# Spreading the transposes, splitting the first products and issuing half of the stores from ScalarE in a convolution with spectral mixing

## The chip, the cores and the metric

The kernel runs on one core of one Trainium2 chip. The metric is the device time of one execution in microseconds. A core has five engines that run their own instruction streams (TensorE for matmuls, VectorE, ScalarE, GpSimd, and SyncE, which issues DMAs here) and 16 DMA engines that move data between the chip's memory (HBM) and the on-chip memory (SBUF). Matmul results are held in PSUM, in 8 banks.

## The reference

The input `x` is float32 of 8 batches x 3264 positions x 192 channels. A causal convolution along the positions (7 taps, softmaxed weights, 8 heads of 24 channels) gives `x'`. A spectral layer keeps the 64 lowest modes, mixes the channels of each mode with a complex 192 x 192 matrix, and goes back. Then comes a residual with a relu:

```python
out = einsum('hk,bskhg->bshg', softmax(weight), windows(x_padded))   # the convolution
X = rfft(out, axis=1)[:, :64]
Yr = Xr @ w_r - Xi @ w_i ;  Yi = Xr @ w_i + Xi @ w_r                 # mode by mode
u = out + irfft(Y, n=S)
result = u + maximum(u @ w_ch, 0)                                    # float32, 8 x 3264 x 192
```

## The kernel before

The 3264 positions are cut into 27 windows of 122 (`WIN`), with 128 rows loaded for each. The whole input is kept in SBUF as bfloat16 (`x_all`), and the convolution overwrites it in place.

Up to about 67 us the kernel loads `x`, convolves it (L243, L250, L252) and computes the 64 modes of the transform by matmuls with a table of sines and cosines, `fst` (L263, L275). All loads are issued by GpSimd[...].

The middle stage is the loop over 16 groups of four modes (`NGRP`, L561). `load_weights(g)` fetches a group's two weight blocks (L234); there are three buffers for this from group 7 on, so that the load of group g + 3 is issued when `mix(g)` is done. `mix(g)` multiplies the modes with the weights (L422) and ScalarE copies the result out (L426). `mix_t(g)` transposes it (L432) into `yeT` (L433). Between the two stands other TensorE work. `t_next` does a pair of chunks of transposes of the convolved input (L389), 22 pairs in all, which VectorE and ScalarE copy to the stashes `cTa` and `cTb` (L393, L395); `make_tail` (L350) prepares the rows for it. `g_part` (L405 to L410) does the same for the sine table and makes `gst`. Groups 0 to 7 have two pairs each, groups 8 to 13 one pair. In front of the mix of group 14 stand four calls of `ab_full` (L469, L474), which begin the accumulation of the first four units in the four PSUM banks of `pza`.

Then `zw_part` (L445) multiplies the mixed modes with the channel matrix, `g_full` (L464) and `relu` (L506) finish the first four units, and the final loop (L610) makes all others. A unit is one window of two batches: `(h, w, k)`, with half `h` of the batches, window `w` and pair `k`. Each unit has a "first half" and a "second half" of its first products on two row tiles of TensorE (`z_ops`, L484), a relu on ScalarE in PSUM (L506), the products of the inverse transform (`y_ops`, L501) and VectorE's addition of `x_all` into an output tile `t` (L536, `finish_unit`). The steps are staggered: at step j of the loop unit j has its first half, j - 2 its second half and relu, j - 4 and j - 5 their `y_ops`, and j - 5 its addition. Each step waits for the PSUM bank of the unit eight before (four before in the first steps). When both pairs of a window and half are added, SyncE stores the tile (L546): 393,216 bytes in rows of 768. There are eight tiles `t` (pool `p3`).

The order of the units is a list: window 0 of the first half, then alternately the next window of the first half and the window before it of the second half:

```python
    wq = [(0, worder[0])]
    for i in range(1, NWIN):
        wq.append((0, worder[i]))
        wq.append((1, worder[i - 1]))
    wq.append((1, worder[-1]))
```

The instructions stand on each engine in the order in which the program writes them.

Of the kernel before, what the change touches and what calls it, by code (L numbers as in the profile page):

```python
# [18 lines left out]
def kernel(  # L19
# [9 lines left out]
    nc = tc.nc  # L29
# [9 lines left out]
    NWIN = 27  # L39
# [5 lines left out]
    NGRP = MODES // MG  # L45
# [17 lines left out]
    def load_unit(b, u):  # L63
# [9 lines left out]
        else:  # L73
# [22 lines left out]
                      in_=bass.AP(tensor=weight.tensor, offset=weight.offset, ap=[[0, P], [1, H * KK]]))  # L96
# [26 lines left out]
    for g in range(4):  # L123
        i0 = OV if g == 0 else 0
        nc.vector.tensor_copy(out=diagc[32 * g:32 * g + 32, i0:NB],
                              in_=diag[32 * g:32 * g + 32, 32 * g - OV + i0:32 * g + 32])
# [46 lines left out]
    for g in range(4):  # L173
        i0 = OV if g == 0 else 0
        dst = cband[32 * g:32 * g + 32, :, 32 * g - OV + i0:32 * g + 32]
# [55 lines left out]
    def load_weights(g, pool):  # L231
        wt = pool.tile([P, MG, 3, D], BF16, tag="wt", name="wt")
        for half, src in ((0, moe_w_r), (1, moe_w_i)):
            nc.gpsimd.dma_start(out=wt[64 * half:64 * half + 64, :, :, :],  # L234
                                in_=src[MG * g:MG * g + MG, :, :].rearrange("m (p j) e -> p m j e", j=3))
        wtiles[g] = wt
# [127 lines left out]
    for p in range(4):  # L364
        k = 0
        for i in range(11):
            n = 8 if i < 4 else 7
# [5 lines left out]
    def ahead(i):  # L373
        for p, k, n in chunks[i:i + 2]:
            w0 = max(k - 2 * NWIN, 0)
            w1 = k + n - 2 * NWIN
            if w1 > w0:
                make_tail(p, w0, w1 - w0)
# [38 lines left out]
    def mix(g):  # L417
        zt = pt.tile([P, 512], F32, tag="p", name="yp")
        for j in range(3):
            for pos in range(4):  # L420
                m = MG * g + pos
                nc.tensor.matmul(zt[32 * pos:32 * pos + 32, 0:D],  # L422
                                 xt[:, j:j + 2, :, m].rearrange("p j k -> p (j k)"), wtiles[g][:, pos, j, :],
                                 start=(j == 0), stop=(j == 2), tile_position=(0, 32 * pos))
        ymix = workp.tile([P, D], BF16, tag="ymix")
        nc.scalar.copy(out=ymix[:], in_=zt[:, 0:D])  # L426
        return zt, ymix
# [34 lines left out]
    def g_full(u, zp, part):  # L462
        h, w, k = u
        nc.tensor.matmul(zp[:, 0:2 * D], gst[:, WIN * w:WIN * w + P], zwi[(h, part, k)], start=False,  # L464
                         stop=(part == 1), skip_group_check=True)

    def ab_full(u, zp):
        h, w, k = u
        nc.tensor.matmul(zp[:, 0:2 * D], xt[:, 3, 0:2, :].rearrange("p a m -> p (a m)"), win0[:, :],  # L469
                         start=True, stop=False, skip_group_check=True)  # L470
        for i in range(2):
            for c0, wv in ((WIN * (NWIN * i + w), win0[:, 0:D]),
                           (WIN * (2 * NWIN + w), (wB0[:, :], win1[:, 0:D])[i])):
                nc.tensor.matmul(zp[:, D * i:D * i + D], cTs[2 * h + k][:, c0:c0 + P], wv,  # L474
                                 start=False, stop=False, skip_group_check=True)
# [29 lines left out]
    def relu(zp):  # L505
        return nc.scalar.activation(out=zp[:, 0:2 * D], in_=zp[:, 0:2 * D], func=ACT.Relu)  # L506
# [24 lines left out]
    def finish_unit(u, zp):  # L531
        h, w, k = u
        if k == 0:
            ts[h] = p3.tile([P, B // 2, D], F32, tag="t", name="t")
        t = ts[h]
        add = nc.vector.tensor_tensor(  # L536
            out=t[:, 2 * k:2 * k + 2, :],
            in0=zp[:, 0:2 * D].rearrange("p (i e) -> p i e", i=2),
            in1=x_all[:, 4 * h + 2 * k:4 * h + 2 * k + 2, w, :], op=ALU.add)
        if k == 0:  # L540
            return
        rows = ((0, 80), (80, LASTVALID)) if w == NWIN - 1 else ((0, P),)
        for r0, r1 in rows:
            dst = bass.AP(tensor=out.tensor, offset=out.offset + (4 * h * S + WIN * w + r0) * D,
                          ap=[[D, r1 - r0], [S * D, B // 2], [1, D]])
            nc.sync.dma_start(out=dst, in_=t[r0:r1, :, :])  # L546


    CH = 7
    worder = sorted(range(NWIN), key=lambda w: (w % CH, w // CH))  # L550
    wq = [(0, worder[0])]
    for i in range(1, NWIN):
        wq.append((0, worder[i]))
        wq.append((1, worder[i - 1]))
    wq.append((1, worder[-1]))
    seq = [(h, w, k) for h, w in wq for k in range(2)]

    ahead(0)
    gq = [0, 1]
    zps = []  # L560
    for g in range(NGRP):  # L561
        last = g == NGRP - 1
        if g == 14:
            assert tpos[0] == len(chunks)
            zps = [pza.tile([P, 512], F32, tag="z", name="z") for _ in range(4)]
            for n in range(4):
                ab_full(seq[n], zps[n])
        m = mix(g)
        if g == 6:
            wts0_stack.close()  # L570
            cTb = ctx.enter_context(tc.tile_pool(name="stashb", bufs=1)).tile([P, CTW], BF16, tag="cTb")
            nc.vector.memset(cTb[:, NSLOT * WIN:CTW], 0.0)
            cTs[3] = cTb[:, :]
        if g in (0, 1, 2):
            load_weights(g + 7, wp)
        elif 7 <= g and g + 3 < NGRP:
            load_weights(g + 3, wp)
        if not last:
            for _ in range(2 if g < 8 else 1):
                t_next(2 if g < 6 else 3)  # L580
            if gq and g % 2 == 1:
                g_part(gq.pop(0))
        mix_t(g, *m)
    early_stack.close()
# [10 lines left out]
    for n in range(2):  # L595
        g_full(seq[n], zps[n], 1)
        finish_unit(seq[n], zps[n])
# [1 line left out]
        g_full(seq[n], zps[n], 0)  # L599
        relu(zps[n])  # L600
    zw_part(1, 1, "vv")
    for n in range(2, 4):
        g_full(seq[n], zps[n], 1)
        finish_unit(seq[n], zps[n])
    ps2.close()
    pzb = ctx.enter_context(tc.tile_pool(name="pzb", bufs=4, space=PSUM))

    N = len(seq)
    zword, yword = {}, {}
    for j in range(4, N + 6):  # L610
        o0, o1 = [], []
        if j < N:
            zps.append((pza if j % 8 >= 4 else pzb).tile([P, 512], F32, tag="z", name="z"))
            o0 = z_ops(seq[j], zps[j], 0)
        if 4 <= j - 2 < N:
            o1 = z_ops(seq[j - 2], zps[j - 2], 1)
        zword[j] = run_pair(o0, o1, zword.get(j - 2))
        if 4 <= j - 2 < N:
            relu(zps[j - 2])
        o0, o1 = [], []  # L620
        if 4 <= j - 4 < N:
            o0 = y_ops(seq[j - 4], zps[j - 4], 0)
        if 4 <= j - 5 < N:
            o1 = y_ops(seq[j - 5], zps[j - 5], 1)
        yword[j - 4] = run_pair(o0, o1, yword.get(j - 5))
        if 4 <= j - 5 < N:
            finish_unit(seq[j - 5], zps[j - 5])

# [1 line left out]
_INS = ['x', 'weight', 'moe_w_r', 'moe_w_i', 'moe_w_ch']  # L630
# [26 lines left out]
```

## Time and profile before

| what | value |
|---|---|
| median of 8 runs | 191.26 us (190.46 to 193.28) |
| the profiled execution | 191.18 us |
| its span, first to last instruction | 189.4 us |
| mean TensorE clock granted | 0.932 |
| TensorE, VectorE, ScalarE, GpSimd busy | 152.4, 126.7, 114.4, 49.3 us |
| issued by GpSimd: DMA packets' time as a share of 16 engines' span | 78.0% |
| issued by SyncE: the same | 36.4% |

The profile is of one execution. The span is shorter than the device time of the same execution by 1.8 us. PE stands for TensorE's matmuls, PEld for its weight loads, DVE for VectorE, ACT for ScalarE, POOL for GpSimd, SP for SyncE, SPq for SyncE's queue of instructions. L546 is line 546 of the kernel as printed above. A DMA share over 1 means that some of the 16 DMA engines had more than one packet in work.

### The profile page before, as it was taken

Reading aid. Unit: us, or ns where it says so; the run is one execution under the profiler, and the core shown is the slowest. Engines: PE = TensorE matmul, PEld = TensorE weight load, DVE = VectorE, ACT = ScalarE, POOL = GpSimd, SP = SyncE. Lnnn points to the kernel's source line nnn. Section 1 sums busy time; section 2 is a strip of 40 time slices with the busy share of each in tenths; the row PEclk is TensorE's granted clock in tenths of the full one; section 3 lists DMA queues with packets and bytes.
Section 4 is the critical chain, followed back from the end, with each engine's and each line's share of the span. In section 5 each row is a group of like instructions: output and inputs, shape, how many; then the busy total and the mean of one; then the engine's idle time right before and its main releaser. Section 6 shows DMA issues by size and latency. Waiting matters only on the chain.

```text
span 189.4 us, 5478 instructions
## 1 busy us (share of the span) xinstructions
PE 152.4 (80%) x2145; PEld 131.3 (69%) x2145; DVE 126.7 (67%) x257; ACT 114.4 (60%) x197; POOL 49.3 (26%) x77
## 2 busy tenths in 40 slices
PE   0637499888899787989849969999999999999800
PEld 0315389777787575868737747899999999998500
DVE  5988965625434358686734408699999999998900
ACT  2049945655575357668643416688888888888600
POOL 7957344332632843421445000000000000000000
PEclk9997969999999999999995599999999999999955
DMA  3999999999999999999999920599999999999996
GB/s 39 164 184 192 192 192 193 192 192 193 192 194 189 162 200 205 207 206 207 186 188 198 205 35 14 158 317 297 322 323 319 320 320 322 322 307 323 301 305 210
DMA packets 65668, 41.59 MB, mean 220 GB/s; under 512 B 30090, under 2 KB 65642, under 8 KB 65642
## 3 DMA queue, kind: packets, MB, share of 16 engines
q0 software_dynamic: 37088, 20.14, 78.0%
q1 hardware_dynamic: 28554, 21.10, 36.4%
q8 instruction: 17, 0.28, 0.5%
q14 instruction: 9, 0.07, 0.1%
HBM read 40.31 MB, written 21.01 MB: 324 GB/s over the span
## 4 chain that ended last, share of the span: by engine, by line
DMA 44%; PE 40%; DVE 4%; ACT 2%; POOL 2%; issue 2%; DVEq 0%; POOLq 0%; ACTq 0%
DMA x_all<-in_x_dram 31%; PE z L484 18%; DMA wt<-in_moe_w_i_dram 13%; PE z L501 13%; PE tp L389 5%; PE yp L422 2%; DVE t L536 2%; POOL wt L234 2%; DVE cTa L393 1%; ACT cTa L395 1%; DVE tail L350 1%; PE zwps L445 1%; ACT z L506 1%; POOL x_all L61 1%; ACT zw L459 0%
## 5 line engine op out<-in xcount | busy, mean ns | idle before, releaser
L536 DVE TENSOR_TENSOR t<-z,x_all 128x384 f32<-128x384 f32 x108 | 59.5, 557 | 4.2 <-PE z L501 2.3
L506 ACT ACTIVATE z<-z 128x384 f32<-128x384 f32 x108 | 51.1, 475 | 12.0 <-PE z L484 2.1
L501 PE MATMUL z<-zw,gst 64*128 64x384 bf16 x208 | 46.5, 323 | 0.2
L484 PE MATMUL z<-zw,gst 64*128 64x384 bf16 x208 | 46.5, 323 | 0.0
L484 PE MATMUL z<-win,cTa 64*128 64x192 bf16 x385 | 42.1, 243 | 0.0
L250 ACT CAST x_all<-cp 122x768 bf16<-122x768 f32 (+2 forms) x34 | 28.4, 876 | 19.3 <-PE cp L243 19.3
L484 PEld LDWEIGHTS <-cTa 64*128 64x128 bf16 x462 | 35.6, 94 | 3.0
L243 PE MATMUL cp<-x_all,cband 128*128 128x240 bf16 (+2 forms) x192 | 24.2, 273 | 10.1 <-DVE kprod L192 3.1
L243 PEld LDWEIGHTS <-cband 128*128 128x128 bf16 x192 | 18.4, 104 | 14.2 <-issue 7.5
L61 POOL DMA_DIRECT2D x_all<-in_x_dram x24 | 22.8, 958 | 19.4 <-DMA x_all<-in_x_dram 18.6
L252 DVE CAST x_all<-cp 122x960 bf16<-122x960 f32 (+2 forms) x14 | 15.0, 1071 | 13.9 <-PE cp L243 13.9
L263 PE MATMUL xp<-x_all,fst 122*128 122x192 bf16 (+1 forms) x216 | 22.2, 252 | 0.9 <-DVE x_all L252 0.5
L263 PEld LDWEIGHTS <-fst 122*128 122x128 bf16 (+1 forms) x216 | 18.4, 100 | 2.1 <-DVE x_all L252 0.7
L484 PEld LDWEIGHTS <-gst 64*128 64x128 bf16 x208 | 19.2, 94 | 0.8 <-issue 0.8
L484 PE MATMUL z<-win,cTb 64*128 64x192 bf16 x135 | 19.5, 243 | 0.0
L484 PE MATMUL z<-wB,cTa 64*128 64x192 bf16 x77 | 18.7, 243 | 0.0
L395 ACT COPY cTa<-tp 128x854 bf16<-128x854 bf16 (+1 forms) x16 | 14.3, 911 | 6.7 <-PE tp L389 6.7
L501 PEld LDWEIGHTS <-gst 64*128 64x128 bf16 x208 | 16.3, 93 | 0.9 <-POOLq L518 0.9
L234 POOL DMA_DIRECT2D wt<-in_moe_w_r_dram x16 | 9.9, 619 | 24.6 <-PE yp L422 15.2
L393 DVE COPY cTa<-tp 128x854 bf16<-128x854 bf16 (+1 forms) x17 | 10.6, 625 | 7.2 <-PE tp L389 6.7
L484 PEld LDWEIGHTS <-cTb 64*128 64x128 bf16 x162 | 14.4, 94 | 1.2
L389 PE MATMUL tp<-ident,x_all 122*128 122x122 bf16 x216 | 14.9, 223 | 0.0
(90 smaller groups left out, 175.2 us busy)
## 6 DMA issues: line engine op xcount, KB each, us to landing
out_dram<-t SPq DMA_DIRECT2D x52, 384.0 KB, 5.1
wt<-in_moe_w_r_dram POOLq DMA_DIRECT2D x16, 288.0 KB, 7.9
wt<-in_moe_w_i_dram POOLq DMA_DIRECT2D x16, 288.0 KB, 8.6
x_all<-in_x_dram POOLq DMA_DIRECT2D x8, 432.0 KB, 15.9
x_all<-in_x_dram POOLq DMA_DIRECT2D x9, 384.0 KB, 17.9
x_all<-in_x_dram POOLq DMA_DIRECT2D x7, 480.0 KB, 18.4
out_dram<-t SPq DMA_DIRECT2D x2, 240.0 KB, 4.2
out_dram<-t SPq DMA_DIRECT2D x2, 36.0 KB
```

The source lines that it names most:

```text
L61: nc.gpsimd.dma_start(out=x_all[:, b, c0:c0 + n, :], in_=src)
L234: nc.gpsimd.dma_start(out=wt[64 * half:64 * half + 64, :, :, :], in_=src[MG * g:MG * g + MG, :, :].rearrange("m (p j) e -> p m j e", j=3))
L243: nc.tensor.matmul(cp[:, j, 0:GRP * n].rearrange("p (w e) -> p w e", w=n), cband[:, h, :], x_all[:, b, w0:w0 + n, GRP * h:GRP * h + GRP], ...
L250: nc.scalar.copy(out=dst, in_=srcv)
L252: nc.vector.tensor_copy(out=dst, in_=srcv)
L263: nc.tensor.matmul(xp[:, 0:D], fst[0:k, c, :], x_all[0:k, b, c, :], start=(c == 0), stop=(c == NWIN - 1))
L389: nc.tensor.transpose(tp[:, WIN * k:WIN * k + WIN], slot_lhsT(p, k0 + k), ident[0:WIN, 0:WIN])
L395: nc.scalar.copy(out=dst, in_=tp[:, 0:WIN * n])
L484: return nc.tensor.matmul(o, lhsT, rhs, start=start, stop=stop, skip_group_check=True, tile_position=(lo, 0))
L501: return [lambda: nc.tensor.matmul(zp[:, 0:2 * D], gst[lo:hi, WIN * w:WIN * w + P], zwi[(h, 1, k)][lo:hi, :], start=False, stop=(r == 1), ...
L506: return nc.scalar.activation(out=zp[:, 0:2 * D], in_=zp[:, 0:2 * D], func=ACT.Relu)
L536: add = nc.vector.tensor_tensor(out=t[:, 2 * k:2 * k + 2, :], in0=zp[:, 0:2 * D].rearrange("p (i e) -> p i e", i=2), in1=x_all[:, 4 * h + ...
```

## The change

It has three parts. The number of pairs of transposes in each group of the middle stage comes from a table, `TPER`, that spreads them over groups 0 to 13, and the two calls of `g_part` come in groups 0 and 2 instead of 1 and 3. Of the four calls of `ab_full`, two come after the mix of group 14. The first half of the batches gets two windows' lead over the second instead of one, and with it the last product and the addition of units 2 and 3 come after the first halves of units 4 and 5. The stores of the second half are issued by ScalarE, three units after their tile is complete; those of the first half stay on SyncE.

```diff
@@ finish_unit
-            nc.sync.dma_start(out=dst, in_=t[r0:r1, :, :])
+            if h == 0:
+                nc.sync.dma_start(out=dst, in_=t[r0:r1, :, :])
+            else:
+                held.append((unit_no[0] + 3, dst, t[r0:r1, :, :]))
+    held = []
+    unit_no = [0]
+
+    def let_go(all_of_them=False):
+        while held and (all_of_them or held[0][0] <= unit_no[0]):
+            _, dst, src = held.pop(0)
+            nc.scalar.dma_start(out=dst, in_=src)
@@ the order of the units
-    wq = [(0, worder[0])]
-    for i in range(1, NWIN):
+    wq = [(0, worder[0]), (0, worder[1])]
+    for i in range(2, NWIN):
         wq.append((0, worder[i]))
-        wq.append((1, worder[i - 1]))
-    wq.append((1, worder[-1]))
+        wq.append((1, worder[i - 2]))
+    wq += [(1, worder[-2]), (1, worder[-1])]
@@ the loop over the groups
+    TPER = (1, 2, 1, 2, 2, 2, 1, 2, 1, 2, 1, 2, 1, 2, 0)
...
-            for n in range(4):
+            for n in range(2):
                 ab_full(seq[n], zps[n])
         m = mix(g)
+        if g == NGRP - 2:
+            for n in range(2, 4):
+                ab_full(seq[n], zps[n])
...
-            for _ in range(2 if g < 8 else 1):
+            for _ in range(TPER[g]):
                 t_next(2 if g < 6 else 3)
-            if gq and g % 2 == 1:
+            if gq and g % 2 == 0:
                 g_part(gq.pop(0))
@@ after zw_part(1, 1, "vv")
-    for n in range(2, 4):
-        g_full(seq[n], zps[n], 1)
-        finish_unit(seq[n], zps[n])
     ps2.close()
...
     for j in range(4, N + 6):
+        if j == 6:
+            for n in range(2, 4):
+                g_full(seq[n], zps[n], 1)
+                finish_unit(seq[n], zps[n])
...
             relu(zps[j - 2])
+        unit_no[0] = j
+        let_go()
...
             finish_unit(seq[j - 5], zps[j - 5])
+    let_go(True)
```

## The prediction

> **What bounds the kernel now.** I read the page's 40 slices first, then a table of stretches over the second half, then the queue of SyncE by itself, then the waits and the chain around the one place where the DMA engines stand still.
>
> The slices, of 4.73 us each, show two long DMA phases with one hole:
>
> ```profile
> PEclk9997969999999999999995599999999999999955
> DMA  3999999999999999999999920599999999999996
> GB/s 39 164 184 192 192 192 193 192 192 193 192 194 189 162 200 205 207 206 207 186 188 198 205 35 14 158 317 297 322 323 319 320 320 322 322 307 323 301 305 210
> ```
>
> Loads fill the DMA engines until about 109 us, stores from 123 us to the end; TensorE's clock is at half in the 22nd and 23rd slice. The stretches give the store phase in numbers (columns: stretch, its length, busy us of each engine with instruction counts, clock, DMA share, GB/s):
>
> ```profile
> core 0: us, PE busy (x) PEld busy (x) DVE busy (x) ACT busy (x) POOL busy (x), PEclk, DMA share, GB/s
> 111.60:117.30 5.70, 4.76 (x52) 3.90 (x53) 3.24 (x8) 3.12 (x8) 0.00 (x0) 1.00 0.02 4
> 117.30:119.30 2.00, 1.92 (x21) 1.21 (x21) 1.90 (x4) 0.35 (x1) 0.00 (x0) 1.00 0.55 166
> 119.30:123.20 3.90, 3.90 (x72) 3.57 (x71) 2.12 (x4) 3.28 (x8) 0.00 (x0) 1.00 0.39 122
> 123.20:141.00 17.80, 17.80 (x315) 16.73 (x312) 17.30 (x32) 14.78 (x32) 0.00 (x0) 1.00 1.02 314
> 141.00:165.00 24.00, 24.00 (x424) 22.55 (x420) 23.37 (x43) 19.91 (x43) 0.00 (x0) 1.00 1.04 321
> 165.00:180.00 15.00, 14.38 (x228) 12.00 (x223) 14.23 (x28) 11.36 (x24) 0.00 (x0) 1.00 1.02 311
> 180.00:188.00 8.00, 0.00 (x0) 0.00 (x0) 0.41 (x1) 0.00 (x0) 0.00 (x0) 0.54 0.99 303
> ```
>
> Compute is done at 180.4, and the DMA engines run on alone for 8 us. So the end is not TensorE's, though the page's chain of waits, which follows instructions, gives it 40%. TensorE makes a unit in 0.57 us, so one store of 393,216 bytes every 1.14 us (344 GB/s); the DMA engines carry one in 1.225 us (at 321 GB/s). The backlog grows until the end. The store queue (packets, MB, its packets' share of 16 engines' span) and the two engines that feed it:
>
> ```profile
> L536 DVE TENSOR_TENSOR t<-z,x_all 128x384 f32<-128x384 f32 x108 | 59.5, 557 | 4.2 <-PE z L501 2.3
> L506 ACT ACTIVATE z<-z 128x384 f32<-128x384 f32 x108 | 51.1, 475 | 12.0 <-PE z L484 2.1
> q1 hardware_dynamic: 28554, 21.10, 36.4%
> out_dram<-t SPq DMA_DIRECT2D x52, 384.0 KB, 5.1
> ```
>
> A packet (one 768-byte row) takes 0.364 x 16 x 189.4 us / 28554 = 38.6 ns, and a DMA share of 1.04 says that an engine has hardly more than one in work. SyncE's own instructions, the first and two later ones:
>
> ```profile
> 117.29 0.40 SPq L546 DMA_DIRECT2D out_dram<-t  x1
> 138.23 1.15 SPq L546 DMA_DIRECT2D out_dram<-t  x1
> 164.12 2.24 SPq L546 DMA_DIRECT2D out_dram<-t  x1
> ```
>
> An issue costs 0.37 to 0.40 us into an empty queue and 1.1 to 2.2 us into a full one. Last, what sets the start of the stores: the last weights (chain of waits), then the pieces around the second window (order of time):
>
> ```profile
> 103.59 7.95 DMA wt<-in_moe_w_i_dram
> 111.68 0.53 PE yp L422 x10
> 117.14 1.13 DVE L456 TENSOR_SCALAR zw<-zwps,ascale 128x384 bf16<-128x384 f32 x2
> 117.33 0.70 PE L464 MATMUL z<-zw,gst 128*128 128x384 bf16 x2
> 118.19 1.01 DVE L536 TENSOR_TENSOR t<-z,x_all 128x384 f32<-128x384 f32 x2
> 118.79 0.34 PE L484 MATMUL z<-zw,gst 64*128 64x384 bf16 x2
> ```
>
> So end = landing of the last weights (111.5) + 10.7 us to the third store (issued 122.2; the two before it leave the DMA engines idle in between) + the stores after it at the DMA rate.
>
> **What the Trainium skill says.** "DMA: Bandwidth & Descriptors", Issuing engines are not separate DMA queues: SyncE's and ScalarE's DMAs run on the same 16 engines and interleave; two issuers save issue time alone. The trace of before has one issuer of stores, so it can't show this. Same page, Why small descriptors are slow: about 3 cycles of overhead to a 256-byte piece (11 cycles). Three pieces to a row and its 850 MHz make 33 cycles, 38.8 ns, an estimate; the 38.6 ns measured agree, which speaks for a limit in the engines, not in the queue. "Perfetto Trace Analysis", DVE / Act Engine Instruction: a compute instruction is pushed to a wait queue and the sequencer goes on; by the same page's section on HWDGE a DMA is executed by the sequencer itself. ScalarE issues no DMA in before, so no line shows it. "TensorE: Matmul & The Clock Gate", What's actually happening: the clock is set in windows of 3.4 us by how busy TensorE was. The trace agrees: it fell at 98.8 us after 3.4 us with TensorE 45% busy (1.5 us of matmuls from 95.4 to 98.8) and rose at 109.0.
>
> **The change part by part.**
>
> *Transposes evened* (t_next: 14 pairs before mix 7 become 11, the three go to groups 9, 11 and 13; g_part one group earlier). Nothing is added. A pair is 1.0 us of TensorE (16 transposes), a mix 0.53, its transposes 0.28, so groups with two pairs need 2.8 us and those with one 1.8, against 2.9 us in which the DMA engines bring a group's weights (mix 10 to 13 start at 96.2, 99.1, 102.0, 104.9). Mix 7 comes up to 3 us earlier, so GpSimd, which waited 6.5 us for it (load at 89.2), issues sooner. That fills two dips in the DMA rate (167 and 175 GB/s at 90 to 92 and 94 to 96, against 206). But the last packets trickle in at 9 GB/s from 110 to 112: a few engines lag and had no dip to fill. I take 0 for the landing of the last weights (bounds -0.5 and 0).
>
> *First products split in two and two* (ab_full). The same 20 matmuls; one half now comes behind mix 14. Mix 15 waits for its weights anyway, at 111.5. Cost 0, if the clock is full; bounds below under the third rival.
>
> *Two windows' lead and g_full of units 2 and 3 moved behind the first halves of units 4 and 5.* Those take 0.83 us (117.96 to 118.79). They now run at 117.3, in place of a wait for relu; both g_full start at 118.15 instead of 117.33 and 117.70, and DVE's addition of unit 2 at about 118.6 instead of 118.19, since it was DVE that held it. Unit 6 needs unit 2's bank, so it starts at 119.2 instead of 118.79: +0.4 us for all that follows, the third store included. The DMA engines stand idle just before that store, so nothing hides it: +0.4 (bounds 0 and +0.6).
>
> *27 windows' stores (28 DMAs) to ScalarE's queue, three units late.* Four relus are 4 x 475 = 1.90 us of ScalarE in 2.29 us of four units. An issue of 0.37 makes 2.27 even if the engine stood still for it. In the full state the 1.13 us would make 3.03, more than the 2.45 that two stores need; but a queue is full only while the DMA engines have work, so this slows compute, not the stores: 0. Behind the issue wait the next relus, and for them y_ops; the relus pushed before it go on. The three units of delay (1.7 us): if the sequencer runs ahead, the store leaves once its addition is done: 0. If not, the third store is done 1.23 us after its start, the next of SyncE comes after 2.29, and the DMA engines idle once for 1.06 us. I take 0 (bounds 0 and +1.06). A second queue keeps engines fed where SyncE hangs for 2.2 us: rates of 314 and 311 instead of 321 in the stretches from 123 and 165 us are worth 17.8 x 0.022 + 15 x 0.031 = 0.9 us; I take -0.3 (bounds -0.9 and 0).
>
> Sum against the profiled execution: 189.4 + 0.4 - 0.3 = 189.5, and with the 1.8 us outside its span (191.18 - 189.4) 191.3. Its own time lies at the median of before, 191.26. What a measurement of this kernel can tell from no change is about 1%, so 189.3 to 193.2 is "same".
>
> **The rivals.**
>
> *Two queues carry more.* For: while loading, packets overlapped (DMA share 1.21 against 1.04 here), so an engine can have more than one in work; a second ring could bring this to the stores. Against: the 38.6 ns is what the engine's cycles give, and the first store, alone in the queue, ran no faster. If the rate passes 344 GB/s, compute is next: 180.4 + 0.4, the last store lands 2.7 us after issue (as the first ones), and about 0.7 for the end: 184.2, or 186.0. Half way, at 335 GB/s, 20.9 MB take 62.4 instead of 65.1 us: 188.6. I put this case at 188.3.
>
> *ScalarE is held.* If each issue holds ScalarE, and also waits while SyncE sits in the descriptor generator (the section on HWDGE has it locked by one issuer at a time), relus fall behind before queues are full; 0.3 us a store for 26 stores is +8 us: 199. Against: ScalarE has 0.39 us to spare in four units, and DMA 8 us of backlog.
>
> *Slower: the clock is at half when the last mixes end.* Place: 109 to 116 us. With the transposes no longer early and only two first products behind mix 14, TensorE has, by my estimate, 1.9 us of work from 109.0 to 112.4 (before: 2.4). If that window counts as idle, the 4.8 us of TensorE work from 111.6 to 117.3 runs at half speed for 3.4 us: +1.7. If the clock falls already by 99, as before, groups of two pairs take 4.7 us instead of 2.9, and mix 15 is late by up to 3.5. With the +0.4: 193.4 to 195.2; I take 194.0. It decides from a window under about half busy: 45% fell, 67% (64.7 to 68.1) did not. For it: 55% by my count. Against: groups 9 to 13 get busier (some 75%).
>
> **How the numbers follow.** Forecast 191.3: chance 0.46 (own range 190.3 to 192.7). Two queues carry more: 0.30. Clock: 0.18. ScalarE held: 0.06. Faster: 0.29 of the first rival and 0.02 of the forecast, 0.31; slower: 0.16 of the clock, 0.06 of ScalarE, 0.03 of the forecast, 0.25; same 0.44. The range leaves out ScalarE's case and the outer parts of the two others: 187.0 to 194.4.
>
> **What would show it.** Right: stores again at 315 to 325 GB/s and 1.04 share in 141 to 165; the third store about 0.4 us later after the last weights; ScalarE issues mostly inside relu time; compute ends before the stores by 6 us or more. Wrong: a share over 1.1 and over 330 GB/s (first rival), ScalarE idle before relus that their products did not hold (second), a clock of 0.5 between 109 and 116 (third).

## The result and the profile after

| | before | after |
|---|---|---|
| median of the runs taken together | 191.70 us (56 runs) | 193.10 us (21 runs) |
| ratio to before, 95% interval | | 1.0112 (1.0084 to 1.0139) |
| the profiled execution | 191.18 us | 192.41 us |
| its span | 189.4 us | 190.5 us |

The ratio compares only the fast runs of each kernel, those within 1.5% of its fastest, so it is not the ratio of the two medians, which is 1.0073. By it the change costs 1.1%, some 2.1 us. The page's slices (4.76 us each here) still show two long DMA phases with one hole, and a TensorE clock that is full from 97.6 us on until compute is done:

```profile
PEclk9999879999999999999879999999999999999975
DMA  3999999999999999999999903499999999999994
GB/s 37 190 190 192 192 195 190 192 195 189 192 193 192 196 202 207 206 205 204 206 160 196 157 2 108 143 300 320 321 314 313 314 319 314 321 315 294 317 283 156
```

The store phase begins 1.8 us earlier than in before (first store issued at 115.52 instead of 117.29 us). Most of that lies ahead of the change: the last packet of `x` landed at 61.1 us instead of 62.6. These are its stretches (stretch, its length, busy us with counts of PE, PEld, DVE, ACT and POOL, clock, DMA share, GB/s):

```profile
117.50:123.00 5.50, 5.50 (x100) 5.03 (x98) 3.55 (x7) 4.32 (x10) 0.00 (x0) 1.00 0.50 156
123.00:141.00 18.00, 18.00 (x320) 16.92 (x317) 17.52 (x33) 14.98 (x32) 0.00 (x0) 1.00 0.98 298
141.00:165.00 24.00, 23.49 (x403) 20.35 (x399) 21.19 (x41) 18.93 (x41) 0.00 (x0) 1.00 1.03 316
165.00:180.00 15.00, 13.33 (x220) 10.46 (x215) 12.63 (x24) 10.05 (x22) 0.00 (x0) 1.00 1.04 308
180.00:188.00 8.00, 1.05 (x5) 0.28 (x4) 1.49 (x3) 0.86 (x2) 0.00 (x0) 0.68 1.01 300
```

The stores run at 316 GB/s in the middle, with a share of 1.03; before it was 321 and 1.04. So the second queue did not raise the rate. Compute, which before was done at 180.4 us, now reaches 182.7. The two engines that feed the stores, and the two queues:

```profile
L536 DVE TENSOR_TENSOR t<-z,x_all 128x384 f32<-128x384 f32 x108 | 58.2, 556 | 9.6 <-PE z L501 4.4
L506 ACT ACTIVATE z<-z 128x384 f32<-128x384 f32 x108 | 50.9, 475 | 16.4 <-PE z L484 4.3
q1 hardware_dynamic: 14430, 10.59, 18.4%
q10 hardware_dynamic: 14124, 10.51, 18.2%
out_dram<-t SPq DMA_DIRECT2D x26, 384.0 KB, 6.7
out_dram<-t ACTq DMA_DIRECT2D x26, 384.0 KB, 6.8
```

The durations of the operations are unchanged (556 and 475 ns), their idle time has grown (9.6 from 4.2 us and 16.4 from 12.0). A packet takes 0.366 x 16 x 190.5 us / 28554 = 39.1 ns instead of 38.6. That is a mean over all packets of the queues; 27360 of the 28554 are rows of 768 bytes, and in the traces these alone take 40.3 ns on average instead of 39.8.

The pieces of the chain around mix 15 and the start of the stores, in order of time (start, length, what), answer to the last lines that the prediction shows of before:

```profile
97.63 5.79 DMA wt<-in_moe_w_i_dram
109.65 0.24 DVE yeT L433
109.90 0.53 PE yp L422 x10
115.52 0.92 PE z L484 x8
116.44 0.28 PE z L464
116.75 0.57 DVE t L536
```

Before, mix 15 (L422) was released by a DMA of weights. Here the chain names `yeT` (L433), the transposed result of mix 14, which ended 0.02 us earlier. But it is the weights again: their last packet landed at 109.43 us and mix 15 starts 0.47 us later, and before it was 111.22 us and 0.46. In all six profiles in which TensorE was free by then (before, after, k2_lead, k4_hold0, k7_end_on_sync, k8_halves) it is 0.45 to 0.47 us. Before, mix 15 even started (111.68 us) before `yeT` of mix 14 was done (111.76), so it does not need it. And `g_full` of unit 2 (L464) now comes behind eight first products (L484), as the change has it.

Then comes what the sum put at nothing. This is the DMA share of 121 to 126 us in 40 slices of 0.125 us, from the DMA view of after:

```profile
DMA  0000039999999993000000019999999999999999
```

The third store's data flow from 121.69 to 122.98 us, and then the DMA engines stand still for 0.98 us, until the fourth store, ScalarE's first, which was issued at 122.94. The same view of before has the third store running straight into the fourth:

```profile
DMA  9982000000000000189999999999999999899999
```

The end is changed too. The two lines are the DMA share of 186 to 189 us in slices of 0.075 us, first before, then after:

```profile
DMA  9999999999999999999999741000000000000000
```

```profile
DMA  9999999999999999889877766443211100000000
```

Before, all 16 DMA engines finish within 0.3 us of each other (by their last packets, 187.66 to 187.92). After, they drop out one by one over 1.3 us (187.24 to 188.52), and all of this is ScalarE's queue: the last data of SyncE's came at 185.33 us. From the last packet to the end of the span it takes 2.0 us instead of 1.5.

Read from the traces, in us, with three of the experiments below beside them:

| | before | after | k6_one_queue | k7_end_on_sync | k10_held_end_on_sync |
|---|---|---|---|---|---|
| third store issued | 122.20 | 120.77 | 121.58 | 122.36 | 122.37 |
| its first data | 123.12 | 121.69 | 122.50 | 123.28 | 123.30 |
| last data | 187.91 | 188.52 | 187.99 | 188.17 | 190.13 |
| third store to last data | 64.79 | 66.83 | 65.49 | 64.89 | 66.83 |
| last data to the span's end | 1.50 | 2.00 | 1.53 | 1.52 | 1.54 |

After against before: -1.43 at the third store, +2.04 from there to the last data, +0.50 at the end, together +1.1 us, the difference of the spans. The gain of 1.43 comes from the load of `x` (1.5 us earlier) and is not the change's. What is left of the loss, 2.5 us, is near the 2.1 us of the times. More can't be asked of single profiles: among the five kernels that store whole tiles on SyncE alone, the distance from the third store to the last data runs from 64.6 us (k2_lead) to 65.5 (k1_transposes, k6_one_queue).

### The profile page after: what moved, and what is told of

It is laid out like the page before. It is cut to its first block, busy times and chain, and to the rows that moved or that the text cites. A ratio compares the mean times of both kernels' runs of the same rounds, so it can differ in the third digit from the quotient of the medians.

```text
span 190.5 us, 5432 instructions
## 1 busy us (share of the span) xinstructions
PE 150.8 (79%) x2145; PEld 127.4 (67%) x2145; DVE 125.1 (66%) x257; ACT 114.3 (60%) x197; POOL 49.4 (26%) x77
## 4 chain that ended last, share of the span: by engine, by line
DMA 49%; PE 31%; POOL 7%; DVE 5%; issue 2%; ACTq 1%; ACT 0%; DVEq 0%; POOLq 0%
DMA x_all<-in_x_dram 26%; DMA wt<-in_moe_w_i_dram 14%; PE z L484 13%; DMA out_dram<-t 9%; PE z L501 8%; PE tp L389 4%; POOL x_all L61 3%; DVE t L536 3%; POOL wt L234 2%; PE yp L422 2%; PE zwps L445 2%; DVE tail L350 1%; ACTq L558 1%; PE z L464 1%; PE z L474 1%
## 5 line engine op out<-in xcount | busy, mean ns | idle before, releaser
L536 DVE TENSOR_TENSOR t<-z,x_all 128x384 f32<-128x384 f32 x108 | 58.2, 556 | 9.6 <-PE z L501 4.4
L506 ACT ACTIVATE z<-z 128x384 f32<-128x384 f32 x108 | 50.9, 475 | 16.4 <-PE z L484 4.3
L501 PE MATMUL z<-zw,gst 64*128 64x384 bf16 x208 | 42.9, 323 | 1.8 <-ACT z L506 1.7
L484 PE MATMUL z<-zw,gst 64*128 64x384 bf16 x208 | 42.8, 323 | 1.8 <-DVE t L536 1.7
L484 PE MATMUL z<-win,cTa 64*128 64x192 bf16 x385 | 41.6, 243 | 0.0
L484 PEld LDWEIGHTS <-cTa 64*128 64x128 bf16 x462 | 33.5, 94 | 4.4
L484 PEld LDWEIGHTS <-gst 64*128 64x128 bf16 x208 | 17.3, 94 | 3.8 <-issue 3.6
L484 PE MATMUL z<-win,cTb 64*128 64x192 bf16 x135 | 19.2, 243 | 0.0
L484 PE MATMUL z<-wB,cTa 64*128 64x192 bf16 x77 | 18.7, 243 | 0.0
L501 PEld LDWEIGHTS <-gst 64*128 64x128 bf16 x208 | 14.8, 94 | 2.6 <-issue 2.0
L484 PEld LDWEIGHTS <-cTb 64*128 64x128 bf16 x162 | 14.1, 94 | 1.6
L389 PE MATMUL tp<-ident,x_all 122*128 122x122 bf16 x216 | 14.2, 218 | 0.0
```

Source lines behind the costliest of these rows:

```text
L389: nc.tensor.transpose(tp[:, WIN * k:WIN * k + WIN], slot_lhsT(p, k0 + k), ident[0:WIN, 0:WIN])
L484: return nc.tensor.matmul(o, lhsT, rhs, start=start, stop=stop, skip_group_check=True, tile_position=(lo, 0))
L501: return [lambda: nc.tensor.matmul(zp[:, 0:2 * D], gst[lo:hi, WIN * w:WIN * w + P], zwi[(h, 1, k)][lo:hi, :], start=False, stop=(r == 1), ...
L536: add = nc.vector.tensor_tensor(out=t[:, 2 * k:2 * k + 2, :], in0=zp[:, 0:2 * D].rearrange("p (i e) -> p i e", i=2), in1=x_all[:, 4 * h + ...
```

## Experiments: each part alone

My theory was that the end is "landing of the weights + start of the stores + stores at the DMA rate", and that the loss sits in the stores: in the three units' delay and in two queues. Rivals: the moved products, the order, or the clock. The first four kernels took the change apart. All ratios here and below are to the kernel before on the same chip, with 95% intervals. The twelve kernels ran on three chips, four on each, so that a comparison of two of them can also be one of two chips.

**k1_transposes**: the kernel before, with this alone:

```diff
+    TPER = (1, 2, 1, 2, 2, 2, 1, 2, 1, 2, 1, 2, 1, 2, 0)
...
-            for n in range(4):
+            for n in range(2):
                 ab_full(seq[n], zps[n])
         m = mix(g)
+        if g == NGRP - 2:
+            for n in range(2, 4):
+                ab_full(seq[n], zps[n])
...
-            for _ in range(2 if g < 8 else 1):
+            for _ in range(TPER[g]):
...
-            if gq and g % 2 == 1:
+            if gq and g % 2 == 0:
```

> The kernel before with the first part of the change alone: the table of transposes, the two calls of g_part one group earlier, and the first products split two and two; order of units and stores as before. Theory A (the loss of the change lies in the stores and their start, the transposes fill dips of the load rate and give a little): 0.2 to 0.8 us faster than before, the last weights land about 0.5 us sooner after the end of the input's load than the 48.6 us of before. Theory B (the transposes themselves cost, by a late mix 15 or a clock at half): slower by 1 us or more, and mix 15 starts over 0.5 us after the landing of its weights.

Measured: 0.9994 (0.9963 to 1.0025); neither the gain nor the loss that was expected shows. First to third store 4.90 us, as before. The weights landed early, 108.78 us, but mix 15 did not start before 110.86, because the first products ahead of it ran at half clock (106.0 to 109.4 us). In this profile TensorE gave back what the loads gained.

**k2_lead**: the kernel before, with the two windows' lead and the moved products alone:

```diff
-    wq = [(0, worder[0])]
-    for i in range(1, NWIN):
+    wq = [(0, worder[0]), (0, worder[1])]
+    for i in range(2, NWIN):
         wq.append((0, worder[i]))
-        wq.append((1, worder[i - 1]))
-    wq.append((1, worder[-1]))
+        wq.append((1, worder[i - 2]))
+    wq += [(1, worder[-2]), (1, worder[-1])]
...
-    for n in range(2, 4):
-        g_full(seq[n], zps[n], 1)
-        finish_unit(seq[n], zps[n])
...
     for j in range(4, N + 6):
+        if j == 6:
+            for n in range(2, 4):
+                g_full(seq[n], zps[n], 1)
+                finish_unit(seq[n], zps[n])
```

> The kernel before with the two windows' lead and the moved last products of units 2 and 3 alone; all stores on SyncE at once. Theory A: the third store starts 0.3 to 0.4 us later after the landing of the last weights (before: 11.9 us), nothing else moves: 0.2 to 0.5 us slower. Theory C (the order of the units costs in the store phase as well): over 1 us slower, with DMA engines idle in places where before had none.

Measured: 1.0037 (1.0001 to 1.0073). First to third store 5.24 us, 0.34 more than before.

**k3_stores**: the kernel before, in its own order, with the stores of the second half on ScalarE, three units late:

```diff
-            nc.sync.dma_start(out=dst, in_=t[r0:r1, :, :])
+            if h == 0:
+                nc.sync.dma_start(out=dst, in_=t[r0:r1, :, :])
+            else:
+                held.append((unit_no[0] + 3, dst, t[r0:r1, :, :]))
...
```

> The kernel before with the stores of the second half on ScalarE, three units late, and its order of units (one window's lead). Theory A (the late first stores of ScalarE leave the DMA engines idle once, and the end is ragged): here it is the third store that is ScalarE's, so the idle time before it grows by about 1 us, and the end adds 0.5 to 1 us: 1.2 to 2.2 us slower than before. Theory D (the queues as such do nothing, the whole change's loss comes from elsewhere): within 0.4 us of before.

Measured: 1.0150 (1.0100 to 1.0200). In this order the third store is ScalarE's; it was issued at 123.26 us, first to third store 6.04 us instead of 4.90. The last data come 1.97 us ahead of the span's end. These are six runs; by the medians of all runs, 193.21 against 191.75 us, the loss is 0.8%. By either, the stores alone lose about as much as the whole change; the intervals of the two overlap.

**k4_hold0**: the changed kernel without the delay:

```diff
-                held.append((unit_no[0] + 3, dst, t[r0:r1, :, :]))
+                held.append((unit_no[0] + 0, dst, t[r0:r1, :, :]))
```

> The whole change with the hold of three units taken away: a store of the second half is issued by ScalarE at the next step of the loop after its tile is complete. Theory A: the idle time of the DMA engines between the third and the fourth store (0.98 us in the trace) shrinks to under 0.2 us, and the time falls by 0.6 to 1.1 us against the whole change, so 1.0 to 1.5 us above before is left. Theory E (the hold is what keeps ScalarE's relus free; without it ScalarE waits for VectorE at each store): relus late by some tenths at every store, compute slower, the time equal to the whole change's or worse.

Measured: 1.0107 (1.0057 to 1.0156), from six runs only, and inconclusive: the experiments below make the delay worth 1.0%, and this interval leaves no room for that, while the medians of all runs (192.70 against 191.75 us) differ by 0.5%. The hole was gone (first to third store 5.19 us, no idle DMA time behind the third), but the profiled execution, the slowest of the six, had another loss. Its stretches of 110 to 118 us and its first `zw_part` (L445):

```profile
110.00:114.00 4.00, 2.25 (x31) 1.71 (x29) 0.45 (x2) 0.42 (x2) 0.00 (x0) 0.98 0.06 10
114.00:118.00 4.00, 4.00 (x27) 3.48 (x25) 1.97 (x4) 2.20 (x5) 0.00 (x0) 0.60 0.01 2
```

```profile
113.42 2.50 PE L445 MATMUL zwps<-win,yeT 128*128 128x192 bf16 x16 [0.39 <-DVE yeT L433]
```

The clock fell to half at 113.8 us, after 3.4 us (110.4 to 113.8) with TensorE 49% busy, and the 16 matmuls that take 1.55 us in the kernel after took 2.50. From the last weights to the first store's data went 8.6 us instead of 7.0. This is the third rival of the prediction, with its place and its price (1.6 us; 1.7 was foretold). Behind the last mix it stands in this profile alone. But ahead of mix 15 the clock was at half for 3.4 us from 105 to 107 us on in five of the nine profiles with evened transposes (k1_transposes, k6_one_queue, k9_one_queue_halves, k10_held_end_on_sync, k12_not_moved), and there too the first data came 8.1 to 8.6 us after the weights.

## Experiments: the delay, the second queue and its end

**k5_split_now**: the kernel before, in its order, with the stores split over two queues as in k3_stores, but `unit_no[0] + 0`.

> The kernel before with the stores of the second half on ScalarE, issued at the next step of the loop, without the hold of three units; order of units and transposes as before. Theory A (the hold costs about 1 us at the start, two queues cost at the end, where the 16 DMA engines finish their last store up to 1.3 us apart instead of 0.3): the third store's data start about 5.0 us after the first store's (before 4.9, with the hold 6.0), the end stays late; 0.5 to 1.3 us slower than before. Theory F (the hold is the whole cost of the split): within 0.3 us of before.

Measured: 1.0059 (1.0023 to 1.0095). The store phase runs at 321 and 320 GB/s in 140 to 155 and 155 to 170 us, where before ran at 320 and 316. Third store to last data is 65.45 us (64.79 before), and the last data come 1.97 us ahead of the span's end (1.50): together +1.1 us. The rates put it at the end, and 1.1 us is also what the ratio says. The DMA share of 185.6 to 188.6 us in slices of 0.075 us:

```profile
DMA  9998998888767655532322221000000000000000
```

The engines drop out over more than 1.8 us, again on ScalarE's queue alone; the last data of SyncE's came at 186.17 us.

**k6_one_queue**: the changed kernel with all stores on SyncE, at once:

```diff
-            if h == 0:
-                nc.sync.dma_start(out=dst, in_=t[r0:r1, :, :])
-            else:
-                held.append((unit_no[0] + 3, dst, t[r0:r1, :, :]))
+            nc.sync.dma_start(out=dst, in_=t[r0:r1, :, :])
...
```

> The whole change without its split of the stores: transposes, first products and order of units as in the changed kernel, all stores on SyncE at once. Theory A: only the later third store is left, 0.2 to 0.6 us slower than before, so 1.5 to 2 us faster than the whole change. Theory G (the transposes and the order cost together what neither does alone): 1 us or more slower than before.

Measured: 0.9938 (0.9907 to 0.9969). Parts one and two together make the kernel faster, which neither expectation had; the stores take back 1.7% (1.0112 against 0.9938), 3.3 us.

**k7_end_on_sync**: as k4_hold0, but the last six windows of the second half are issued by SyncE too:

```diff
-            if h == 0:
+            if h == 0 or w in worder[-6:]:
```

> The whole change without the hold, and with the second half's stores of the last six windows on SyncE, so that one queue is left in the last 14 us. Theory A: the DMA engines finish their last store within 0.4 us of each other and the time from the last packet to the end of the span is again 1.5 us (2.0 in the changed kernel): equal to the whole change without its split within 0.3 us, 0.3 to 0.6 us slower than before. Theory H (two queues cost in every stretch, not at the end): 0.8 us or more slower than before, with a lower rate from 125 to 170 us.

Measured: 0.9969 (0.9930 to 1.0008). The engines end within 0.7 us of each other, and the last data come 1.52 us ahead of the end. ScalarE's queue has had its last data by 176.85 us here. That this is better than one queue throughout is not shown (0.9969 against 0.9938).

**k10_held_end_on_sync**: the same, but with the three units' delay kept (`unit_no[0] + 3`), so that it differs from k7_end_on_sync by the delay alone.

> The changed kernel with its three units' delay kept, and the last six windows of the second half issued by SyncE. It differs from the same kernel without the delay (ratio 0.997) by the delay alone. If the delay costs its idle time: 0.9 to 1.0 us more, a ratio of 1.001 to 1.003, with a hole of about 1 us in the DMA work ahead of ScalarE's first store, and 1.5 us from the last packet to the end of the span as with one queue. If the delay is only another face of two queues at the end: 0.997 again.

Measured: 1.0066 (1.0039 to 1.0093). The two intervals do not touch: the delay costs 1.0%, 1.9 us, with an interval of about 0.9 to 2.8 us for the difference. k3_stores and k5_split_now, the same pair in the order of before, differ by 0.9%. ScalarE's own order of time (start, length, engine, line) around the first store that it issues, first in k7_end_on_sync, then in k10_held_end_on_sync:

```profile
121.67 2.13 ACT L506 ACTIVATE z<-z 128x384 f32<-128x384 f32 x4 [0.16 <-PE z L501]
123.56 0.42 ACTq L558 DMA_DIRECT2D out_dram<-t  x1
```

```profile
121.68 3.28 ACT L506 ACTIVATE z<-z 128x384 f32<-128x384 f32 x6 [0.16 <-PE z L501]
124.54 0.51 ACTq L558 DMA_DIRECT2D out_dram<-t  x1
```

From mix 15 on the two executions differ by no more than 0.01 us up to here. Without the delay the issue already stands behind the relu of the next step, so the three units' delay moves it two steps on in the program, and that is where it goes in the trace: two relus further on, 0.98 us later. The sequencer of ScalarE does not run ahead of its relus to it. In all 21 issues of k10_held_end_on_sync, and in the first 21 of the 28 of after, the issue starts 0.06 us after the start of the relu in front of it (122.94 and 122.88 us for the first of after). The DMA share of 122 to 127 us (slices of 0.125 us) with the delay, then without:

```profile
DMA  0000000000599999999820000000299999999999
```

```profile
DMA  0000000000699999999889999999999999999999
```

With the delay the engines stand still for 0.98 us. The distance from the third store to the last data grows by more, 66.83 against 64.89 us: 1.94. The remaining 0.96 us is a lower rate in this pair of profiles. The stretches of 155 to 170 and 170 to 180 us, again with the delay, then without:

```profile
155.00:170.00 15.00, 14.30 (x245) 11.51 (x242) 12.29 (x24) 11.45 (x25) 0.00 (x0) 1.00 1.03 316
170.00:180.00 10.00, 9.17 (x156) 7.34 (x151) 8.59 (x17) 7.35 (x16) 0.00 (x0) 1.00 1.03 302
```

```profile
155.00:170.00 15.00, 15.00 (x269) 14.56 (x266) 14.62 (x27) 12.34 (x27) 0.00 (x0) 1.00 1.04 320
170.00:180.00 10.00, 9.30 (x144) 7.82 (x138) 9.22 (x19) 7.33 (x16) 0.00 (x0) 1.00 1.04 310
```

With the delay VectorE has 12.29 us of work in 15 us instead of 14.62: tiles stay occupied longer, and compute falls to the pace of the stores sooner. The engines stay busy all the same (1.03), but the stores run at 316 and 302 GB/s instead of 320 and 310. That the delay does this is not shown: k6_one_queue, which has no delay, runs at 316 and 295 in the same two stretches, and before at 316 and 314. With the delay ScalarE's issue comes 0.1 us ahead of SyncE's, so that the stores start in twos; without it they alternate at 1.1 to 1.2 us. Whether that makes the packets slower was not tried apart. So the hole is the delay's for certain, 1.0 us, and what fills the rest of the 1.9 us is open.

**k11_all_on_scalar**: all stores on one queue, but ScalarE's; the kernel is k6_one_queue with `nc.scalar` for `nc.sync` at the store.

> As the changed kernel, but all stores issued by ScalarE, without delay: one queue, on the other engine. If one queue is what makes the end even: the 16 DMA engines finish within 0.3 us of each other, 1.5 us before the span's end, and the time is that of all stores on SyncE (ratio 0.994) as long as ScalarE has time for 54 issues. If it matters that the queue is SyncE's: 1.3 us apart and 2.0 us, ratio 1.00 to 1.005. If full queues hold ScalarE (1.1 to 2.2 us for an issue, 2 x 1.1 + 4 x 0.475 = 4.1 us in the 2.45 us of two stores at the worst), relus fall behind and the DMA engines run dry: 1.05 or more.

Measured: 1.0101 (1.0068 to 1.0133). The end agrees with "one queue": fifteen of the sixteen engines finish within 0.2 us of each other (189.90 to 190.06 us), the rows of the last go on to 190.67, and that is 1.51 us ahead of the span's end. So ScalarE's queue by itself gives neither the ragged end nor the longer final wait; both go with two queues. One reserve stands: the engines had run dry shortly before here, which may have evened them too. The loss is elsewhere. The stretches from 140 us, and ScalarE in order of time:

```profile
140.00:155.00 15.00, 14.47 (x236) 10.99 (x232) 12.87 (x24) 10.05 (x24) 0.00 (x0) 1.00 1.00 307
155.00:170.00 15.00, 14.63 (x241) 11.23 (x238) 13.21 (x24) 10.30 (x24) 0.00 (x0) 1.00 1.02 313
170.00:180.00 10.00, 8.69 (x144) 6.63 (x142) 7.81 (x14) 6.01 (x14) 0.00 (x0) 1.00 0.89 270
```

```profile
129.68 0.86 ACT L506 ACTIVATE z<-z 128x384 f32<-128x384 f32 x2 [0.47 <-PE z L484]
130.43 0.38 ACTq L546 DMA_DIRECT2D out_dram<-t  x1
130.86 0.86 ACT L506 ACTIVATE z<-z 128x384 f32<-128x384 f32 x2 [0.32 <-PE z L501]
131.76 0.38 ACTq L546 DMA_DIRECT2D out_dram<-t  x1
```

Between two relus and the next two stands an issue of 0.38 us, which waits for its addition; the products behind wait for the relus, and the relus then for the products (0.47 and 0.32 us). A tile leaves every 1.27 us (third to 38th store, 121.74 to 166.12 us) instead of every 1.14, so compute has no backlog to give the engines, and from 170 us on they run dry (share 0.89). Compute ends at 187.7 instead of 180.4 us. That is the second rival, ScalarE held, at twice the issues of the change; it is worth 1.6% here (1.0101 against 0.9938), not the 4% that was feared, and only two of the issues took much longer than 0.5 us (0.89 and 1.34 us).

## Experiments: the order and a better version

**k8_halves**: the kernel before, its first four tiles stored in two pieces of two batches, each as soon as its pair is added:

```diff
-        if k == 0:
+        early = (h, w) in first
+        if k == 0 and not early:
             return
...
+            b0, nb = (2 * k, 2) if early else (0, B // 2)
-            nc.sync.dma_start(out=dst, in_=t[r0:r1, :, :])
+            nc.sync.dma_start(out=dst, in_=t[r0:r1, b0:b0 + nb, :])
...
+    first = wq[:4]
```

> Not a part of the change but what it points to: the kernel before with the first four tiles stored in two pieces of two batches each, as soon as each pair is added, all on SyncE. If the store phase is bound by the DMA engines from the third store on, the third store's data start 0.57 us earlier after the first store and the whole ends 0.3 to 0.6 us sooner than before. If the end were set by TensorE, no change within 0.2 us.

Measured: 0.9949 (0.9913 to 0.9984), faster than before by 1 us.

**k9_one_queue_halves**: the same edit in k6_one_queue.

> All parts of the change but the second queue, and the first four tiles stored in two pieces of two batches each. If the time is last weights + start-up to the first data + stores at the DMA rate, then the half tiles let data flow about one unit (0.5 to 0.6 us) earlier and fill part of the idle time before the third store: together with the 0.6% of all stores on SyncE a ratio of 0.989 to 0.992, and last minus third data no longer the right measure, but less DMA idle time between the first and the fifth piece. If smaller pieces cost the DMA engines as much as they save: 0.994, as without them.

Measured: 0.9904 (0.9863 to 0.9946), 1.8 us faster than before. That it is better than k6_one_queue is not shown: the intervals overlap, and the medians of all runs are 0.55% and 0.46% under those of before. The DMA share of 117 to 127 us in slices of 0.25 us, k6_one_queue and then k9_one_queue_halves:

```profile
DMA  0999991000899991000000999999999999999999
```

```profile
DMA  2008950019936999920000029999999995079999
```

Half tiles fill a part of the two holes between the first stores, and open a small one (0.3 us at 125.5 us) where the whole tiles begin.

**k12_not_moved**: k6_one_queue with the last products and additions of units 2 and 3 back ahead of the loop.

> All stores on SyncE, evened transposes and the two windows' lead, but the last products and additions of units 2 and 3 left where they were, ahead of the loop. If the moved products cost the 0.34 us that the distance from first to third store shows (4.90 against 5.24): that distance is 4.9 again and the ratio 0.991 to 0.993, 0.2% under that of the kernel with them moved. If the order of the units brought the 0.6% and not the start: no difference beyond 0.1%. If units 6 and 7 now wait for something else: distance 5.2, ratio 0.994.

Measured: 0.9941 (0.9908 to 0.9974), first to third store 4.90 us. The distance is back at that of before, as the step said, but the time does not show it: 0.34 us are 0.18%, and these intervals are 0.3% to each side. So whether the moved products cost what the distance says stays open.

That k1_transposes (0.9994) and k2_lead (1.0037) gain nothing alone while both together gain 0.6% was not settled. The profile of k6_one_queue doesn't show the gain: its span is 189.5 us, that of before 189.4. Its weights landed early, at 108.72 us, but its stretches of 102 to 110 us show why the stores did not start earlier by as much:

```profile
102.00:106.00 4.00, 1.76 (x30) 1.50 (x31) 2.64 (x7) 1.98 (x3) 0.56 (x1) 0.91 1.21 207
106.00:110.00 4.00, 4.00 (x43) 3.31 (x40) 0.92 (x3) 1.19 (x2) 0.00 (x0) 0.66 0.61 102
```

TensorE was busy for 1.76 of 4 us, the clock fell at 105.3 us, and the work ahead of mix 15 ran at half clock. The first store's data came 8.5 us after the weights instead of 7.0. In the 3.4 us before the clock fell TensorE had been 44% busy here, 49% in k4_hold0 and 45% in before. How often this happens in the executions that were not profiled is not known, so it can't be said whether the gain in the times is that of the runs without it.

## Why the prediction was right and wrong

The forecast was 191.3 us, no change. Measured is a median of 193.10 us, +1.1% by the ratio: inside the range of 187.0 to 194.4, at the upper edge of what was called "same" (to 193.2), and above the forecast's own range of 190.3 to 192.7. That it came so near is in part luck. The stores cost some 3 us where -0.3 stood, and a gain of 1.2 us from the other two parts, which I had not foretold, took back a part of it.

- *What bounds the kernel.* Right. In all kernels but k11_all_on_scalar, where the engines run dry, the end is the start of the stores plus the stores at 295 to 323 GB/s, with a DMA share of 0.98 to 1.05 (140 to 180 us).
- *Moved products, +0.4.* Right in size: first to third store 5.24 us against 4.90 in each kernel that has them moved (k2_lead, k6_one_queue, k7_end_on_sync), and 4.90 without (k1_transposes, k12_not_moved). The third store is issued 11.34 us after the last weights in after, k2_lead and k7_end_on_sync, 10.98 in before. Too small to be seen in the times.
- *Three units' delay, 0 (bounds 0 and +1.06).* This step failed. The step gave the right alternative, "if not, the third store is done 1.23 us after its start, the next of SyncE comes after 2.29, and the DMA engines idle once for 1.06 us", and took the wrong branch, with the sequencer running ahead. Measured: 0.98 us of standing still, in after and in k10_held_end_on_sync. I had taken from the Trainium skill's "Perfetto Trace Analysis", DVE / Act Engine Instruction, that the sequencer pushes a compute instruction and goes on; I read this as running ahead by as many relus as one likes. The runs show an issue starting with the relu just in front of it (122.88 and 122.94 us). The hole itself fits the upper bound of 1.06 us. The times give 1.9 us for the term, so the bound was probably too low; what the rest is stays open.
- *Second queue, -0.3 (bounds -0.9 and 0).* The wrong sign. The rates of 314 and 311 GB/s were no dips that a second queue fills: k5_split_now gained 4 GB/s at most between 140 and 170 us and lost 1.1 us over all, 0.66 to the last data and 0.47 from there. The Trainium skill's "DMA: Bandwidth & Descriptors", Issuing engines are not separate DMA queues, had it right for the rate: 321 and 320 GB/s with two queues, 320 and 316 with one. The even finish of one queue was what I didn't ask for.
- *Transposes evened, 0.* Right in the time by itself (0.9994). But the weights did come earlier, by 0.8 us on the mean, more than the bound of 0.5: from the last packet of `x` to the last weights 46.6 to 48.7 us in the nine profiles with this part, 47.8 to 48.9 in the five without. Where they came earliest nothing is left of it at the third store, for TensorE was late, or slow, by then.
- *First products two and two, 0.* Right in after: mix 15 starts 0.47 us after the last packet of its weights, as in before (0.46). Where the clock was at half it starts later (2.1 us after the weights in k1_transposes), as the term's "if the clock is full" had it.
- *Rivals.* Two queues carry more: false (share 1.03, 316 GB/s); in its sum 20.9 MB should have been 20.2, which is what is left behind the second store. Clock at half: real, seen behind the last mix in k4_hold0 and ahead of mix 15 in five others, not the cause in after, whose clock is full from 97.6 us. ScalarE held: its mechanism shows in the end of after, where two issues fill 1.9 us and a relu comes late by as much,

```profile
178.42 1.87 ACTq L558 DMA_DIRECT2D out_dram<-t  x2
180.34 0.47 ACT L506 ACTIVATE z<-z 128x384 f32<-128x384 f32 x1 [1.94 <-DVE t L536]
```

  but the DMA engines are busy there (share 1.04), so that it costs little. Compute ended 5.8 us before the last data; "6 us or more" had been foretold.

In sum, from the times: the delay 1.9 us and two queues about 1.1 us (k5_split_now) in the place of -0.3, against the 1.2 us that the other two parts gain in k6_one_queue, make +1.8 us; measured are 2.1. The agreement is better than the intervals warrant, and in the two profiles alone the stores cost less, 1.34 us to the last data and 0.47 from there (after against k6_one_queue).

## What to carry to other kernels

A DMA issue that is written behind compute instructions on an engine leaves, here, with the one just in front of it: count the delay from there as real when it comes before the DMA engines have a backlog. A second issuing engine does not widen a store phase that already keeps the DMA engines busy, and it can make its end ragged; if issues must be split, bring the last ones back to one queue. Before pulling loads forward, look at what the consumer does in that stretch, for a gain in landing is lost again when TensorE is late or has lost its clock.

## What the runs showed of the hardware

- In the four kernels with stores on two queues to the end the last packets of the 16 DMA engines lie 1.1 to 1.9 us apart (k4_hold0 1.1, after 1.3, k3_stores 1.4, k5_split_now 1.9), in the seven with all stores on SyncE 0.2 to 0.5 us. Where two queues give way to SyncE's for the last 11 us, it is 0.7 (k7_end_on_sync, k10_held_end_on_sync). In each of the four SyncE's queue is done 1.9 to 3.2 us before ScalarE's, so the ragged end is that of one queue left over from two; what makes it so is open.
- From the last data to the span's end: 1.96 to 2.0 us in these four, 1.5 us in the eight other kernels with whole tiles, 1.24 us in the two with half tiles (k8_halves, k9_one_queue_halves). What makes the difference is not seen in the trace.
- The clock of TensorE followed how busy it had been. Between 55 and 170 us of the fourteen profiles it fell to half 15 times, each time after a stretch of 3.4 us (counted from its own changes) with TensorE 40 to 53% busy, and it stayed full after every stretch with 54% or more. Transposes counted: with 55% of transposes and 13% of other matmuls it stayed full (k6_one_queue, from 74.6 us).
